# Three of the eight blocks of a second matmul computed from split operands, with GpSimd taking the difference

## The chip, the cores and the metric

The kernel runs on one core of a Trainium2 chip. The metric is the device time in microseconds (us) of one execution, the median of several runs; lower is better.

## The reference

Three stages follow one another. A gated linear attention with complex decay makes 3072 rows of 384 numbers. A dense mixture turns each row x into `(h * cos(h)) @ w_out` with `h = x @ w_in`. A second mixture sends each row to the one of eight experts that has the largest logit.

```python
def _moe_ref(x, w_in, w_out):
    h = x @ w_in                    # 384 -> 2048
    g = h * np.cos(h)
    return (g @ w_out).astype(np.float32)   # 2048 -> 384
...
    logits = x @ w_gate
    e_idx = np.argmax(logits, axis=1)
...
        h = np.maximum(x[mask] @ w1[e], 0.0)
        ye = h @ w2[e]
        out[mask] = gate_w[mask, None] * eom[mask, e, None] * ye
```

The change touches `g @ w_out`, the second matmul of the first mixture. Its output also feeds an argmax, so it is computed close to full fp32 precision.

## The kernel before

**Units.** The 3072 rows are worked in 12 units u = 0 to 11 of 256 rows. For each unit the kernel runs a scan (`scan`, on VectorE with ScalarE's help: `normal`, `core`, `inverse`, `post`), the attention (`attn`, TensorE with VectorE), and the first mixture. The loop over units interleaves them: while unit u is in the mixture, `attn(u + 1)` and `scan(u + 2)` are pulled forward piece by piece. Units 10 and 11 have no scan left to run, and unit 11 no attention. After unit 11 the experts follow (`second`).

**The mixture of one unit** has eight steps s = 0 to 7, each 256 of the 2048 columns. Step s does:

- `mm1(u, s)` (L508): h for these columns, 18 matmuls with a moving tile of 256 columns. Both operands are split there already, each into a high part in the reduced type fp32r and a low part, and three products are added (high*high, high*low, low*high). The PSUM tile h has two buffers.
- `act2(u, s)` (L516 to L518): three ScalarE activations from h to the SBUF tile g, 128 x 512.
- `act3(u, s)` (L523): VectorE makes g ready, reading g from SBUF and h from PSUM. After it the buffer of h is free, so `mm1(u, s + 2)` waits for it.
- `mm2(u, s - 2)` (L534): the second matmul, two steps later. For two halves of 128 rows and two groups of 128 columns it multiplies g by wo, 4 matmuls in plain fp32 with 400 moving columns (384 outputs and 16 logits); the trace shows each as two records, 8 in a block.

After the last block of a unit, `evac` (L557) copies the sums out, and one unit later `routing` finds each row's expert and scatters the rows with four indirect DMAs on GpSimd's queue (L541).

**GpSimd** does little before the change: once per unit twelve small operations on the carried state (`gates`, L204 and L344 to L353, right after the last operation of `core`), the scatters, and in the first 90 us eight subtractions that split w_in (`split`, the tile wi).

**Order.** A scheduler with a model of times sets the order on each engine from the order of the program and priorities (`tc.high_priority`); each engine then runs its list strictly in that order. Tiles come from pools with a fixed number of buffers: the pool gx, which holds g, has five.

Of the kernel before, what the change touches and what calls it, by code (L numbers as in the profile page):

```python
# [10 lines left out]
F32 = mybir.dt.float32  # L11
F32R = mybir.dt.float32r
# [10 lines left out]
C = 128  # L23
NCB = S // C
NCH = B * NCB
UC = 2
NU = NCH // UC
UPB = NCB // UC
NT = B * S
DM = H * D  # L30
DFF = 2048
KF = DFF // 128
NE = 8
NL = 2 * NE
# [6 lines left out]
NO = DM + NL  # L41
# [5 lines left out]
KP = KF // 2  # L47
NWC = 2 * KP + 1
NB = 2 * NU + 2 * NWC + NU * KF // 2 + NE
MAXH = 39.0  # L50
LAST = 6
EARLY = 5
# [82 lines left out]
def build(tc, ap, out, force=False):  # L135
# [4 lines left out]
    def pool(name, bufs=1, **kw):  # L140
        return tc.tile_pool(name=name, bufs=bufs, **kw)
# [4 lines left out]
    moe_ctx = ExitStack()  # L146
    wp = moe_ctx.enter_context(pool("wp", side="right"))
    xp = moe_ctx.enter_context(pool("xp", 2, side="right"))
    gx = moe_ctx.enter_context(pool("gx", 5, side="right"))
    rowp = moe_ctx.enter_context(pool("rowp", 2, side="right"))  # L150
    attn_ctx = ExitStack()
    qkrp = attn_ctx.enter_context(pool("qkrp", 2, side="left"))
# [50 lines left out]
    def tt(e, o, a, b, op):  # L203
        return e.tensor_tensor(out=o, in0=a, in1=b, op=op)  # L204
# [293 lines left out]
    NS = KF // 2  # L498
# [22 lines left out]
    def act3(u, s):  # L521
        g = gxt[u, s]
        V.scalar_tensor_tensor(out=g, in0=g, scalar=1.0, in1=hps.pop((u, s)), op0=SUB, op1=MUL)  # L523

    def mm2(u, s):
        g = gxt.pop((u, s))
        if s == 0:
            o_t[u] = [ps_o.tile([128, 512], F32, name=f"o{j}") for j in range(UC)]
        for j in range(UC):
            o = o_t[u][j][:, 0:NO]  # L530
            for i in range(2):
                f = 2 * s + i
                cs = slice(j * C, (j + 1) * C)
                PE.matmul(o, lhsT=g[:, i, cs], rhs=wos[s][:, i], start=f == 0, stop=f == KF - 1)  # L534

    rows_t = {}
    scat = {"xs": [], "xs0": [], "out": []}
# [16 lines left out]
    def evac(u):  # L554
        rows_t[u] = rowp.tile([128, UC, ROW], F32, name="rows")
        for j in range(UC):
            mark["evac"] = A.activation(out=rows_t[u][:, j, 0:NO], in_=o_t[u][j][:, 0:NO], func=AF.Copy, scale=-1.0)  # L557
        G.tensor_copy(rows_t[u][:, :, NO].bitcast(I32), ids[:, u * UC:(u + 1) * UC])
# [117 lines left out]
    def split(j):  # L676

        if j < KP:
            w = wp.tile([128, 2, 3, 256], F32R, name="wi", tag=f"w{j}")
            wis[j] = w  # L680
            t = wraw[j][0][..., 0].bitcast(F32)
            hi, lo = (w[:, r].rearrange("p a c -> p (a c)") for r in range(2))
            A.copy(hi, t)
            tt(G, lo, t, hi.bitcast(F32), SUB)
        else:
            w = wp.tile([128, 2, NO], F32, name="wo", tag=f"w{j}")
            wos[j - KP] = w
            if len(wraw[j]) == 1:
                r = wraw[j][0].rearrange("p (i c) t -> p i c t", i=2)
                parts = [(w[..., 0:DM], r[..., 0]), (w[..., DM:NO], r[:, :, 0:NL, 1])]  # L690
            else:
                parts = [(w[:, i, 0:DM], wraw[j][i][..., 0]) for i in range(2)]
                parts += [(w[:, i, DM:NO], wraw[j][i][:, 0:NL, 1]) for i in range(2)]
            for w, t in parts:
                A.copy(w, t.bitcast(F32))

    def gated(j):

# [26 lines left out]
    def run(g):  # L725
        for _ in g:
            pass
# [452 lines left out]
    if True:  # L1180
        load_a(0)
        SY.dma_start(ident, ap["cst"])
        SY.dma_start(cb, ap["msk"])
        SY.dma_start(smt, ap["sm"])
        SY.dma_start(ids, ap["ids"])
        SY.dma_start(rkt, ap["rk"])
        SY.dma_start(wg, ap["wg"].rearrange("(k p) l -> p k l", p=128))
        V.memset(pv_t, 0.0)
        V.tensor_copy(acc, smt[:, 1, 0])
        G.tensor_copy(top, smt[:, 3])  # L1190
        V.memset(eb, 0.0)
        V.memset(one[:, 0], 1.0)
        V.memset(one[:, 1], 0.0)
        nl = 11
        load_w(0, 1)
        load_qk(0)
        load_w(1, nl)
        n0 = 3

        run(scan(0))  # L1200
        load_w(nl, 2 * KP)
        run(weights(range(n0)))
        with tc.issue_after(mark["add", 0].ins):
            run(weights(range(n0, n0 + 2)))
        with tc.issue_after(mark["post", 0].ins):
            run(weights(range(n0 + 2, KP)))
        run(normal(1))
        run(attn(0))
        run(weights(range(KP, KP + EARLY)))
        with tc.high_priority(offset=100):  # L1210
            run(core(1))
            run(inverse(1, None))
        with tc.high_priority(offset=100):
            run(post(1))
        for u in range(NU):
            ga = attn(u + 1) if u + 1 < NU else iter(())
            gs = scan(u + 2) if u + 2 < NU else iter(())
            if u == 0:
                run(ga)
                gs = chain((normal(2), scan(2)))  # L1220

            def pull(g, n):
                for _ in range(n):
                    if next(g, StopIteration) is StopIteration:
                        return

            if u == NU - 2:
                scan_ctx.close()
            if u == NU - 1:
                attn_ctx.close()  # L1230
                open_early()
                for i in range(4):
                    stage(0, i)
                gs = split_w(0)
                gf = None

            for s in range(NS):
                mm1(u, s)
                if u == 0 and s >= EARLY:
                    with tc.issue_after(mark["add", 1].ins):  # L1240
                        run(weights([KP + s]))
                pull(ga, 2)
                pull(gs, 1)
                i = u * NS + s - 2
                if i >= 0:
                    mm2(*divmod(i, NS))
                    if i % NS == NS - 1:
                        with tc.high_priority(offset=300):
                            evac(i // NS)
                act2(u, s)  # L1250
                pull(ga, 1)
                pull(gs, 3)
                with tc.high_priority(offset=50):
                    act3(u, s)
                if s == 4 and u > 2:
                    routing(u - 1)
                    if u == NU - 1:
                        gf = first_half()
                if u == NU - 1 and s >= 4:
                    next(gf)  # L1260
                if s == NS - 1 and 0 < u < 3:
                    routing(u - 1)
            run(ga)
            run(gs)
        for s in range(NS - 2, NS):
            mm2(NU - 1, s)
        with tc.high_priority(offset=300):
            evac(NU - 1)
        with tc.high_priority(offset=100):
            routing(NU - 1)  # L1270
        run(gf)
        moe_ctx.close()
        ps_ctx.close()
        second()
# [21 lines left out]
```

## Time and profile before

| | |
|---|---|
| Median of 3 runs | 987.12 us (986.64 to 987.8) |
| Profiled execution, its own time | 988.75 us |
| Profiled execution, span from first to last instruction | 986.9 us |
| Busy in the span: TensorE / VectorE / ScalarE / GpSimd | 906.4 / 649.9 / 562.1 / 140.8 us |
| L534, second matmul of the first mixture | 768 records, 279.4 us busy |
| L508, first matmul of the first mixture | 1728 records, 250.8 us busy |
| Mean granted TensorE clock | 0.995 of full speed |

Busy time is a sum over the instructions of an engine. TensorE's instructions overlap, and their ends are modelled, so the durations of its records are longer than the time from one to the next; what a matmul costs is read from the chain of waits, where every piece ends where the next begins.

### The profile page before, as it was taken

To read this page: it belongs to the slowest core of one execution; us is meant where nothing else is said; L and a number is where in the kernel's file an instruction comes from. 1 tells how busy PE (TensorE), PEld (TensorE's weight loads), DVE (VectorE), ACT (ScalarE), POOL (GpSimd) and SP (SyncE) were. 2 spreads that over 40 slices of the span, in tenths; PEclk is the share of its full clock that TensorE was granted. 3 is DMA by queue.
4 is the path that set the end of the run, shared out by engine and by line. 5 is a ranking of instruction groups with operands and counts; after the bars stand their busy time and mean duration, and the time that the engine had idled before them with its cause. 6 is when DMAs were issued, how large, how long until landed. Compare 5 with 4: busy or idle time off the path is not lost.

```text
span 986.9 us, 16112 instructions
## 1 busy us (share of the span) xinstructions
PE 906.4 (92%) x5689; PEld 754.8 (76%) x5689; DVE 649.9 (66%) x1466; ACT 562.1 (57%) x1217; POOL 140.8 (14%) x254
## 2 busy tenths in 40 slices
PE   0467899999989999999999999999999999999997
PEld 0356677767768787778787777787789899999997
DVE  6988877696869796878889787334244554255521
ACT  6584875837484947586766655335454454255521
POOL 1122001002022002011212021101111110212101
PEclk9999999999999999999999999999999999999999
DMA  9713135336323333232424141342217542454101
GB/s 325 305 34 93 40 107 188 85 96 212 106 70 119 76 99 86 89 98 84 113 73 113 68 134 26 93 139 87 79 34 255 164 160 61 143 179 141 34 13 35
DMA packets 69790, 109.93 MB, mean 111 GB/s; under 512 B 14064, under 2 KB 51328, under 8 KB 69429
## 3 DMA queue, kind: packets, MB, share of 16 engines
q1 hardware_dynamic: 62724, 98.72, 32.3%
q0 software_dynamic: 6976, 10.10, 3.0%
q8 instruction: 47, 0.77, 0.3%
q14 instruction: 43, 0.34, 0.1%
HBM read 74.20 MB, written 21.86 MB: 97 GB/s over the span
## 4 chain that ended last, share of the span: by engine, by line
PE 43%; DVE 26%; ACT 10%; issue 8%; DMA 7%; SPq 6%; POOL 0%; DVEq 0%; ACTq 0%; POOLq 0%
PE p L933 11%; PE h L918 10%; PE o L534 9%; PE h L508 7%; DVE t L204 4%; DVE qkt L204 4%; DVE l_t L204 2%; DVE g L523 2%; DVE pt L204 2%; DVE nt L204 1%; SPq L368 1%; DMA qkr<-qkt 1%; DMA a_t<-in_a_dram 1%; ACT g L516 1%; SPq L371 1%
## 5 line engine op out<-in xcount | busy, mean ns | idle before, releaser
L534 PE MATMUL o<-wo,g 128*128 128x400 f32 x768 | 279.4, 505 | 0.5 <-ACT rows L557 0.5
L508 PE MATMUL h<-x,wi 128*128 128x256 f32 x1728 | 250.8, 297 | 19.5 <-DVE g L523 11.7
L508 PEld LDWEIGHTS h<-x,wi 128*128 128x128 f32 x1728 | 220.5, 192 | 40.7 <-DVE g L523 12.2
L534 PEld LDWEIGHTS o<-wo,g 128*128 128x128 f32 x768 | 138.4, 191 | 85.9 <-issue 4.1
L933 PE MATMUL p<-w2t,hh 128*128 128x384 f32 (+4 forms) x672 | 131.7, 341 | 0.0
L918 PE MATMUL h<-xe,w1t 128*128 128x384 f32 (+6 forms) x576 | 118.5, 349 | 0.0
L922 DVE SCALAR_TENSOR_TENSOR hh<-h,hh 128x384 fp32r<-128x384 f32 (+6 forms) x64 | 37.2, 583 | 121.1 <-ACT hh L921 121.1
L933 PEld LDWEIGHTS p<-w2t,hh 128*128 128x128 f32 (+4 forms) x672 | 114.0, 179 | 3.6 <-ACT hh L921 0.4
L516 ACT ACTIVATE g<-h 128x512 f32<-128x512 f32 x96 | 57.1, 595 | 104.7 <-PE h L508 104.4
L921 ACT ACTIVATE hh<-h 128x384 fp32r<-128x384 f32 (+6 forms) x64 | 32.8, 514 | 128.0 <-PE h L918 119.5
L918 PEld LDWEIGHTS h<-xe,w1t 128*128 128x128 f32 x576 | 101.7, 188 | 5.2
L523 DVE SCALAR_TENSOR_TENSOR g<-g,h 128x512 f32<-128x512 f32 x96 | 65.5, 682 | 57.0 <-ACT g L518 53.1
L541 POOL DMA_INDIRECT xs<-rows,si x46 | 53.1, 1154 | 195.4 <-DVE si L588 88.8
L518 ACT ACTIVATE g<-g 128x512 f32<-128x512 f32 x96 | 61.1, 636 | 2.0
L437 PE MATMUL sc<-qkr 96*128 96x128 f32 x384 | 55.7, 291 | 5.1 <-DMA qkr<-qkt 5.0
L437 PEld LDWEIGHTS sc<-qkr 96*128 96x128 f32 x384 | 50.8, 203 | 12.3 <-issue 5.1
L517 ACT ACTIVATE g<-h 128x512 f32<-128x512 f32 x96 | 57.7, 601 | 1.9
L541 POOL DMA_INDIRECT out_dram<-o,tok x28 | 35.4, 1265 | 145.7 <-ACT o L943 81.4
L204 POOL TENSOR_TENSOR fg<-l_t,m 128x12 f32<-128x12 f32 x24 | 4.6, 213 | 326.5 <-DVE l_t L204 248.3
L204 DVE TENSOR_TENSOR t<-l_t,a_t 128x192 f32<-128x192 f32 x144 | 46.7, 363 | 1.5
L707 PE MATMUL o<-ident,raw 128*128 128x128 f32 x30 | 8.4, 435 | 37.1 <-DVE raw L665 36.6
L204 DVE TENSOR_TENSOR qkt<-l_t,qk_t 128x1536 f32<-128x1536 f32 (+1 forms) x26 | 41.2, 1631 | 0.2
(277 smaller groups left out, 1351.0 us busy)
## 6 DMA issues: line engine op xcount, KB each, us to landing
stg<-in_w_dram SPq DMA_DIRECT2D x32, 768.0 KB
qkr<-qkt SPq DMA_DIRECT2D x96, 146.2 KB
a_t<-in_a_dram SPq DMA_DIRECT2D x12, 768.0 KB
qk_t<-in_qk_dram SPq DMA_DIRECT2D x12, 768.0 KB
xs<-in_xz_dram SPq DMA_DIRECT2D x17, 401.0 KB
raw<-in_w_in_dram SPq DMA_DIRECT2D x7, 768.0 KB
raw<-in_w_out_dram SPq DMA_DIRECT2D x7, 768.0 KB
vt<-in_v_dram SPq DMA_DIRECT2D x24, 192.0 KB
```

Source lines behind the costliest of these rows:

```text
L204: return e.tensor_tensor(out=o, in0=a, in1=b, op=op)
L437: PE.matmul(sc[:, h], lhsT=t[:, h, 1, 0:C], rhs=t[:, h, 0, 0:C], start=True, stop=True)
L508: PE.matmul(h[:, i], lhsT=wis[s][:, wi, kk, i * 128:(i + 1) * 128], rhs=x_t[u][:, xi, kk], start=n == 0, stop=n == 8)
L516: A.activation(out=g, in_=h, func=AF.Square, accum_out=hck[:, u * NS + s:u * NS + s + 1])
L517: mark["sin"] = A.activation(out=g, in_=h, func=AF.Sin, scale=0.5)
L518: A.activation(out=g, in_=g, func=AF.Square, scale=float(np.sqrt(2.0)))
L523: V.scalar_tensor_tensor(out=g, in0=g, scalar=1.0, in1=hps.pop((u, s)), op0=SUB, op1=MUL)
L534: PE.matmul(o, lhsT=g[:, i, cs], rhs=wos[s][:, i], start=f == 0, stop=f == KF - 1)
L541: sc = G.indirect_dma_start(in_offset=None, oob_is_err=False, **kw)
L918: PE.matmul(h, lhsT=w[:, wi, kk, f * 128:(f + 1) * 128], rhs=x[:, xi, kk], start=n == 0, stop=n == 8)
L922: mark["rest"] = V.scalar_tensor_tensor(out=hh[:, 1], in0=h, scalar=0.0, in1=hh[:, 0].bitcast(F32), op0=ALU.max, op1=SUB)
L933: mm = PE.matmul(o2[e][j][0:w_, 0:DM], lhsT=hh[:, hi, j * w_:(j + 1) * w_], rhs=w[:, wi, f], start=f == 0 and n == 0, stop=f == KE - 1 and ...
```

## The change

Blocks 2, 4 and 6 of each unit take the split path. A new step `act4`, one step after `act3`, copies g to a high part `ghi` in fp32r on ScalarE and lets GpSimd subtract it from g, which gives the low part `glo`. The weights of these three blocks are split as well, once, with VectorE making the low part. In `mm2` each of the 4 matmuls of such a block becomes three: high*high, high*low and low*high. The pool gx gets a sixth buffer; ghi and glo come from it too.

```diff
+SPLIT = (2, 4, 6)
...
-    gx = moe_ctx.enter_context(pool("gx", 5, side="right"))
+    gx = moe_ctx.enter_context(pool("gx", 6, side="right"))
...
+    def act4(u, s):
+
+        if s in SPLIT:
+            g = gxt[u, s]
+            hi = gx.tile([128, 2, UC * C], F32R, name="ghi", tag="g")
+            lo = gx.tile([128, 2, UC * C], F32R, name="glo", tag="g")
+            A.copy(hi, g)
+            tt(G, lo, g, hi.bitcast(F32), SUB)
+            gxt[u, s] = hi, lo
...
-                PE.matmul(o, lhsT=g[:, i, cs], rhs=wos[s][:, i], start=f == 0, stop=f == KF - 1)
+                if s not in SPLIT:
+                    PE.matmul(o, lhsT=g[:, i, cs], rhs=wos[s][:, i], start=f == 0, stop=f == KF - 1)
+                    continue
+                for n, (p, wi) in enumerate(((0, 0), (0, 1), (1, 0))):
+                    PE.matmul(o, lhsT=g[p][:, i, cs], rhs=wos[s][:, wi, i], start=f == 0 and n == 0,
+                              stop=f == KF - 1 and n == 2)
...
+            for i, c, t in parts:
+                A.copy(w[:, i, c], t.bitcast(F32))
+                if two:
+                    tt(V, wl[:, i, c], t.bitcast(F32), w[:, i, c].bitcast(F32), SUB)
...
+                if i >= -1:
+                    with tc.high_priority(offset=50):
+                        act4(*divmod(i + 1, NS))
                 act2(u, s)
```

On TensorE, in unit 8 of the changed kernel (o_5379 and o_5380 are the two halves of its output), a split block stands between two runs of the first matmul:

```order
L509 MATMUL h<-x,wi 128x256 x18
L549 MATMUL o_5379<-wo,ghi 128x400 x2
L549 MATMUL o_5379<-wo,glo 128x400
L549 MATMUL o_5379<-wo,ghi 128x400 x2
L549 MATMUL o_5379<-wo,glo 128x400
L549 MATMUL o_5380<-wo,ghi 128x400 x2
L549 MATMUL o_5380<-wo,glo 128x400
L549 MATMUL o_5380<-wo,ghi 128x400 x2
L549 MATMUL o_5380<-wo,glo 128x400
L509 MATMUL h<-x,wi 128x256 x18
```

Every block of the kernel before has in this place two rows of two matmuls that read g; the order of the blocks is the same.

On ScalarE, the end of one scan (`inverse` is `qkt<-l_t`, `qkt<-nt` and `qkt<-qkt`; `put_gates`, which opens `post`, is `qkt<-fg`) against the steps of the mixture, in unit 9 of the kernel before, right after the evacuation of unit 8:

```order
L557 ACTIVATE rows<-o_5086 128x400
L243 ACTIVATE qkt<-l_t 128x1536
L516 ACTIVATE g,hck<-h 128x512
L517 ACTIVATE g<-h 128x512
L247 ACT_TABLE_LOAD
L247 ACTIVATE qkt<-nt 128x768
L518 ACTIVATE g<-g 128x512
L248 ACTIVATE qkt<-qkt 128x768
L465 CAST x<-pv_t 128x4x128
L357 COPY qkt<-fg 128x24
```

and in unit 9 of the changed kernel, where the copy to ghi is that of block 6:

```order
L244 ACTIVATE qkt<-l_t 128x1536
L517 ACTIVATE g,hck<-h 128x512
L518 ACTIVATE g<-h 128x512
L248 ACT_TABLE_LOAD
L248 ACTIVATE qkt<-nt 128x768
L519 ACTIVATE g<-g 128x512
L249 ACTIVATE qkt<-qkt 128x768
L532 CAST ghi<-g 128x512
L517 ACTIVATE g,hck<-h 128x512
L518 ACT_TABLE_LOAD
L518 ACTIVATE g<-h 128x512
L358 COPY qkt<-fg 128x24
```

The end of this scan has moved from steps 1 to 3 of unit 9 to its steps 5 to 7. In units 2 to 4 the last operation of `core` stands after `act3` of step 6 in the changed order, in unit 9 after that of step 5; before, it went from step 5 in units 2 and 3 to step 1 in unit 9.

On GpSimd, from the end of the gates in unit 5 of the changed kernel to the start of the next gates:

```order
L354 COPY fg<-fg 128x6
L205 TENSOR_TENSOR glo<-g,ghi 128x512
L574 COPY rows<-ids 128x2
L205 TENSOR_TENSOR glo<-g,ghi 128x512 x2
L557 DMA xs<-rows,si 4096x401
L557 DMA xs_122<-rows,si 256x401
L557 DMA xs<-rows,si 4096x401
L557 DMA xs_122<-rows,si 256x401
L205 TENSOR_TENSOR fg<-l_t,m_132 128x12 x2
```

Before, `rows<-ids`, the gates and the four scatters were all that stood there. The subtractions of blocks 2 and 4 now stand ahead of the scatters and the gates, that of block 6 behind them.

## Rows read from the trace of the kernel before

**Rows 1.** Busy time by stage: start:end, length, busy us (x instructions) by engine, clock, DMA.

```profile
0.00:95.00 95.00, 44.35 (x214) 37.22 (x214) 80.15 (x138) 62.66 (x138) 19.50 (x25) 1.00 0.56 196
95.00:284.00 189.00, 171.21 (x1107) 135.42 (x1108) 143.18 (x324) 122.42 (x258) 18.73 (x60) 0.97 0.37 112
284.00:637.00 353.00, 346.47 (x2365) 271.68 (x2364) 282.74 (x652) 226.07 (x483) 53.26 (x119) 1.00 0.32 92
637.00:730.00 93.00, 93.00 (x558) 70.30 (x556) 31.29 (x81) 44.53 (x103) 8.16 (x10) 1.00 0.25 86
```

**Rows 2.** The chain of waits by line: stage 95:284, then 284:637, then 637:730.

```profile
by line: issue 8.3%; PE h L508 6.9%; DVE t L204 5.9%; DMA a_t<-in_a_dram 5.7%; PE o L534 5.2%; DMA xs<-in_xz_dram 3.9%; DVE qkt L204 3.4%; ACT g L516 3.0%; DVE g L523 2.6%; DMA ss<-s__2050 2.5%; DMA ss<-s__831 2.5%; ACT g L517 2.5%; SPq L49
...
by line: issue 10.6%; DVE qkt L204 7.9%; PE o L534 7.7%; DVE t L204 6.4%; PE h L508 5.5%; DVE g L523 5.0%; DVE l_t L204 4.1%; DVE pt L204 3.1%; DMA qkr<-qkt 2.7%; SPq L368 2.6%; DVE nt L204 2.6%; SPq L371 2.0%; ACT L517 1.8%; SPq L488 1.6%;
...
by line: PE o L534 52.6%; PE h L508 34.8%; PE sc L437 3.8%; PE pv_t L456 2.3%; PE pv_t L461 2.3%; PE m L472 1.4%; PE h L870 0.8%; PE sc L422 0.7%; PE sc L852 0.7%; PE m L422 0.6%; PE m L604 0.1%; PE m L585 0.1%; PE m L582 0.0%; PE m L584 0.
```

**Rows 3.** Pieces of that chain: start, us on the chain, engine, tile, line.

```profile
679.84 2.12 PE h L508 x18
681.96 2.69 PE o L534 x8
...
897.09 1.64 PE h L918 x9
```

**Rows 4.** Timeline of TensorE at 897 us, the shape of the piece at 897.09.

```profile
896.93 1.80 PE L918 MATMUL h<-xe,w1t 128*128 128x400 f32 x9
```

**Rows 5.** Waits over the whole span: us in total, times, longest.

```profile
DVE g L523 <- ACT g L518: 53.1, 27, 5.4
...
PE h L508 <- DVE g L523: 11.7, 5, 4.7
```

**Rows 6.** Timeline: gates of the scans 4 and 11, first activation of units 3 and 10.

```profile
271.51 0.20 POOL L344 COPY eb<-l_t 128x12 f32<-128x12 f32 x1
...
599.70 0.20 POOL L344 COPY eb<-l_t 128x12 f32<-128x12 f32 x1
...
283.58 0.58 ACT L516 ACTIVATE g<-h 128x512 f32<-128x512 f32 x1
...
636.93 0.60 ACT L516 ACTIVATE g<-h 128x512 f32<-128x512 f32 x1 [2.83 <-PE h L508]
```

**Rows 7.** Timeline of GpSimd: four of its eight subtractions for wi.

```profile
15.21 2.21 POOL L204 TENSOR_TENSOR wi<-raw,wi 128x768 fp32r<-128x768 f32 x1 [9.13 <-ACT wi L683]
...
26.75 1.99 POOL L204 TENSOR_TENSOR wi<-raw,wi 128x768 fp32r<-128x768 f32 x1 [1.25 <-ACT wi L683]
...
82.95 1.87 POOL L204 TENSOR_TENSOR wi<-raw,wi 128x768 fp32r<-128x768 f32 x1 [1.95 <-ACT wi L683]
85.86 1.85 POOL L204 TENSOR_TENSOR wi<-rawx,wi 128x768 fp32r<-128x768 f32 x1 [1.04 <-ACT wi L683]
```

**Rows 8.** Timeline of VectorE at three of these subtractions.

```profile
15.63 3.40 DVE L204 TENSOR_TENSOR a_t<-a_t,nt 128x1536 f32<-128x1536 f32 x1
...
27.07 1.88 DVE L204 TENSOR_TENSOR l_t<-t 128x192 f32<-128x192 f32 x1
...
87.02 1.10 DVE L204 TENSOR_TENSOR tp<-s__452,ss 96x384 f32<-96x384 f32 x1
```

**Rows 9.** VectorE's operations by tile: durations min/median/max in ns, first and last start.

```profile
L204 DVE TENSOR_TENSOR a_t<-a_t,nt x12: 1750/1758/3402, 15.6 to 572.9; 128x1536 f32<-128x1536 f32 x12
...
L204 DVE TENSOR_TENSOR l_t<-t x84: 341/357/1883, 23.4 to 588.3; 128x192 f32<-128x192 f32 x84
...
L204 DVE TENSOR_TENSOR tp<-s__508,ss x1: 544/544/544, 141.1 to 141.1; 96x384 f32<-96x384 f32 x1
...
L204 DVE TENSOR_TENSOR nt<-a_t,nt x12: 946/954/960, 6.7 to 548.8; 128x768 f32<-128x768 f32 x12
```

**Rows 10.** ScalarE's copies of a 128 x 512 tile from SBUF to fp32r, by tile.

```profile
L766 ACT CAST w1t<-stg x48: 610/622/628, 675.3 to 929.3; 128x512 fp32r<-128x512 f32 x48
```

**Rows 11.** Timeline of VectorE: a small two-operand operation.

```profile
764.90 0.18 DVE L204 TENSOR_TENSOR ex<-rt,pick 128x32 f32<-128x32 f32 x1
```

More of the change, by code (lines that the diff above doesn't have):

```diff
@@ L685, in split @@
         else:
-            w = wp.tile([128, 2, NO], F32, name="wo", tag=f"w{j}")
+            two = j - KP in SPLIT
+            w = wp.tile([128, 2, 2, NO], F32R, name="wo", tag=f"w{j}") if two else wp.tile([128, 2, NO], F32, name="wo", tag=f"w{j}")
             wos[j - KP] = w
+            if two:
+                wl, w = w[:, 1], w[:, 0]
             if len(wraw[j]) == 1:
                 r = wraw[j][0].rearrange("p (i c) t -> p i c t", i=2)
-                parts = [(w[..., 0:DM], r[..., 0]), (w[..., DM:NO], r[:, :, 0:NL, 1])]
+                parts = [(slice(0, 2), slice(0, DM), r[..., 0]), (slice(0, 2), slice(DM, NO), r[:, :, 0:NL, 1])]
             else:
[L692 to L695, printed above, removed]
+                parts = [(i, slice(0, DM), wraw[j][i][..., 0]) for i in range(2)]
+                parts += [(i, slice(DM, NO), wraw[j][i][:, 0:NL, 1]) for i in range(2)]
+            for i, c, t in parts:
+                A.copy(w[:, i, c], t.bitcast(F32))
+                if two:
+                    tt(V, wl[:, i, c], t.bitcast(F32), w[:, i, c].bitcast(F32), SUB)
     def gated(j):
@@ L1264, in build @@
             run(gs)
+        act4(NU - 1, NS - 1)
         for s in range(NS - 2, NS):
```

## The prediction

> **What bounds the kernel now.** I read the table of stages first. TensorE is busy for 44 of the first 95 us, for 171 of the next 189 (units 0 to 2), for 346.5 of 353 in units 3 to 9, and for all 93 us of units 10 and 11 [rows 1]. A full row of busy time does not yet say that TensorE sets the end, so I read the chain of waits by line next. In 637:730 it is TensorE and nothing else, L534 alone holding 52.6%. In 284:637 it is mixed: L534 has 7.7% and L508 5.5%, and the rest is mostly VectorE's scan (the tiles qkt, t, l_t, nt) with ScalarE and DMA. In 95:284 it is mixed too, L534 having 5.2% [rows 2]. The reader should see two things: from unit 10 on, time taken off L534 comes off the end one for one; before that, TensorE and the loop through VectorE are about equally long, since both are nearly without slack.
>
> How much slack the scan has in units 3 to 9 can be read from two pairs of starts. Its gates come at 271.51 and seven scans later at 599.70, so one scan takes 46.9 us; the first activations of units 3 and 10 are at 283.58 and 636.93, so one unit takes 50.5 us [rows 6]. The scan ran 3.6 us faster per unit than the mixture, and got ahead.
>
> **The change, part by part.**
>
> *TensorE.* A block of L534 takes 2.69 us on the chain [rows 3]. Twelve fp32r matmuls take its place. The expert with 400 rows gives the price directly: nine matmuls of L918 with a moving tile of 128 x 400 [rows 4] take 1.64 us on the chain [rows 3], 0.182 each, so 12 take 2.19 us. Each split block saves 0.50 us, 36 of them 18.0 us, if TensorE sets the end everywhere. L508 keeps its 2.12 us [rows 3]. The Trainium skill (FP8 and Floating Point Precision, TensorE Precision Notes) counts four passes for true FP32; three products in place of four passes would save a quarter, an estimated 0.67 us a block and 24 us in all. The rows say less, and the sum goes by the rows.
>
> Where the saving lands:
>
> - Units 10 and 11, 6 blocks: the chain is TensorE alone, so 3.0 us come off in full.
> - Units 3 to 9, 21 blocks: 10.5 us if the scan keeps up, nothing if it doesn't.
> - Units 0 to 2, 9 blocks: 4.5 us of work, but L534 is 5.2% of that stage's chain, 9.8 us [rows 2]. Three of eight of its blocks by 0.50/2.69 is 0.7 us; I take 0.5.
>
> *ScalarE.* 36 copies of 128 x 512 at 0.62 us [rows 10] are 22 us. ScalarE is busy for 226 of 353 us in units 3 to 9 [rows 1]; with 21 copies, 13 us, it stays under 70%. The copy must wait for `act3` on VectorE and holds up the next step's activations behind it. But those wait for the next `mm1`, whose end is a run of L508 and a block of L534 after that of the last, 4.8 us [rows 3], and in the units with attention more. I cost the copies at nothing. If that cover is gone, they cost up to their 0.62 each, 13 us in units 3 to 9.
>
> *GpSimd.* The trace has no subtraction of 512 elements. One of 768 took 1.85 to 1.87 us where little stood against it [rows 7], so by size 1.25 us, and with a fixed part rather more; I take 1.3 us, 47 us in all. GpSimd is busy for 53 of 353 us in units 3 to 9 [rows 1], and 27 more fit. Its list is strict, so `glo` stands in line: those of blocks 2 and 4 ahead of the scatters and the gates, that of block 6 behind them in unit 5. The block that needs it comes behind the L508 run of step s + 2, which itself waits for `act3` of step s. If TensorE is already waiting there, as it did five times [rows 5], 2.12 us of L508 [rows 3] cover 0.62 + 1.3 = 1.9 us of copy and subtraction; otherwise a block and a run more, 4.8 us, lie between. I cost the queue at nothing; what is late first, if this cover is gone, is block 6, behind the gates.
>
> *VectorE, the hidden price.* While GpSimd subtracts, VectorE's operations with two SBUF inputs stand still. The product a_t at 15.63 took 3.40 us where its median is 1.76, ending after the subtraction that began at 15.21; the sum l_t at 27.07 took 1.88 where its median is 0.36, ending with the one that began at 26.75; the product tp at 87.02 took 1.10 against 0.54 [rows 7 to 9]. Over the eight subtractions, the first and last of which are shown, VectorE lost 8.75 us by such excess, in 17.1 us of GpSimd's work: half of it. The Trainium skill (SBUF — State Buffer on-chip working memory, Who interferes with whom) has the rule behind it: a VectorE instruction with two SBUF inputs and a GpSimd instruction that reads SBUF exclude each other, and the second to issue blocks until the first is done. The trace agrees.
>
> So a `glo` of 1.3 us costs VectorE 0 (when it is waiting anyway, or reads PSUM) to 1.3 us; I take half, 0.65. That is 2.0 us in each unit that still has a scan, 19.5 us over units 0 to 9. VectorE is busy for 283 of 353 us in units 3 to 9 [rows 1], 40.4 us of each 50.5; it would be 42.4 of about 49. Part of this falls into time in which it now waits, 53 us in all for ScalarE ahead of L523 [rows 5]. Of the 14 us in units 3 to 9 between 0 and 14 can reach the end; the scan's lead of 3.6 us per unit is the nearest row and is larger than 2.0 plus the 1.5 that TensorE gains, though barely. And the order shows that the scan is given that lead no more: it ends in step 6 or 7 of each unit. I take 30%, 4.2 us.
> In units 0 to 2 the scan has no lead. Nine subtractions cost VectorE 5.9 us there, of which 0 to 5.9 reach the end. VectorE's lines that the rows of 284:637 still show are 29% of that chain, with many small ones cut off [rows 2]; I take 40% of the 5.9, 2.3 us.
>
> *The split weights.* Three more operations of 128 x 768 on VectorE at 0.95 us [rows 9] and three small ones at 0.18 [rows 11], 3.4 us, before and in unit 0, where VectorE is busy for 80 of 95 us [rows 1]. Between 0 and 3.4 us reach the end; I take a little over half, 1.9.
>
> *The sixth buffer* costs nothing: a split block draws three buffers, but each is given back by a matmul or a subtraction that is over before the sixth draw after it.
>
> **The sum.** -3.0 - 10.5 + 4.2 - 0.5 + 2.3 + 1.9 = -5.6 us. Against the profiled execution's own 988.75 us that is 983.1; the median stands 1.6 us below that execution, so **981.5 us**.
>
> **The rivals.**
>
> *All of it arrives.* The scan's waits shrink as fast as the lock lengthens it, and TensorE sets the pace from unit 3: the 4.2 is gone and half of the 4.2 us of early costs too, -11.9 us, about **975**. For it: TensorE is busy for 98% of units 3 to 9. Against it: the chain there runs over VectorE.
>
> *The lock makes VectorE the bound.* From unit 0 to 9 nothing of TensorE's saving counts, and the loop through VectorE grows. Its place is the scan in step 3 (`normal`, then `core`), 5 and 7 of each unit, where nearly every operation has two SBUF inputs; it decides when lock and other additions exceed the scan's lead, 3.6 us a unit, less the 1.5 us by which the mixture speeds up: 2.1 us, and I already expect 2.0. With VectorE on 40% of the chain, 40% of 19.5 us is 7.8; with 1.9 for the weights and -3.0 from the last two units it comes to +6.7 us, **994**. For it: the chain [rows 2], and L508 already waits 11.7 us for L523 [rows 5]. Against it: VectorE is only 80% busy.
>
> *They cancel.* Saving and lock are of one size in units 0 to 9, and what the last two units gain goes to the weights: **987**, within 0.2%.
>
> *The split is not cheaper.* If the matmuls took turns with weight loads worse than those of L918 do, a block would stay at 2.69 us and only the costs would remain, about 995. L918 loads new weights for each of its matmuls too, so this gets little.
>
> **How the numbers follow.** 0.2% is 2.0 us, about what a measurement of this kernel can tell from no change. The forecast's case (977 to 985) gets 0.46, all of it arriving 0.16, cancelling 0.14, VectorE as the bound 0.22, the split that is not cheaper 0.02. So faster is 0.62, same 0.14, slower 0.24. The range runs from 973 (all arrives, and units 0 to 2 give a little) to 994 (the lock as the bound); the likeliest case's own range is 977 to 985.
>
> **What would show it.** Right: L549 at about 2.19 us per split block on the chain; 36 subtractions of 1.3 to 1.7 us on GpSimd; operations such as t<-l_t,a_t and l_t<-t with maxima near 1.7 us all through 100 to 630 us, and VectorE's busy share in units 3 to 9 up from 80% to about 86%; one unit of the mixture at 49.5 to 50 us. Units 10 and 11 together 3 us shorter. Wrong: TensorE waiting for L524 or for qkr by several us per unit in units 3 to 9, gates that come 51 us apart or more, or matmuls of L549 that wait for glo behind the gates.

## The result: 0.7% slower, and the profile after

The median of 8 runs is 993.8 us (992.63 to 996.4), beside 987.8 of the kernel before on the same chip: a ratio of 1.0069, 95% interval [1.0055, 1.0082], so 6.8 us slower (here and below a ratio is turned into us on the 987.1 of before). The forecast was 981.5, 5.6 us faster than before, with a range up to 994: the time lies just inside the range, and the direction is wrong. The profiled execution took 996.2 us itself.

The head of the page, then busy time by stage as in [rows 1]:

```profile
span 994.3 us, 16481 instructions
...
PE 901.7 (91%) x5833; PEld 789.8 (79%) x5833; DVE 670.7 (67%) x1472; ACT 581.6 (58%) x1255; POOL 190.6 (19%) x290
```

```profile
0.00:95.00 95.00, 44.33 (x214) 37.11 (x214) 82.32 (x142) 63.06 (x138) 21.46 (x25) 1.00 0.57 195
95.00:284.00 189.00, 170.45 (x1141) 146.28 (x1142) 149.94 (x322) 128.91 (x268) 31.01 (x67) 0.95 0.37 111
284.00:637.00 353.00, 337.31 (x2400) 284.14 (x2400) 284.69 (x644) 228.01 (x493) 78.51 (x140) 0.98 0.31 87
637.00:730.00 93.00, 91.05 (x596) 76.55 (x595) 38.96 (x85) 51.75 (x114) 18.49 (x18) 0.98 0.33 107
```

In 284:637 TensorE stands idle for 15.7 us where it stood 6.5, and its granted clock is 0.98 instead of 1.00; VectorE is busy for 20.8 us more over the span (649.9 before). Busy time on the page is not the sum of the durations: time in which two instructions of an engine overlap counts once. The pieces of the chain of waits in unit 11 (start, us on the chain) have both kinds of block side by side, as in [rows 3]:

```profile
691.28 2.69 PE o L546 x8
...
696.20 2.18 PE o L549 x12
698.38 2.12 PE h L509 x18
```

The price of a split block was right, 2.18 us for 2.19. (By the four passes that the Trainium skill counts, FP8 and Floating Point Precision, TensorE Precision Notes, it would have been an estimated 2.02; the rows gave the price, not the count.) The new operations by tile (min/median/max in ns), and then one of the scan's small ones, before and after:

```profile
L205 POOL TENSOR_TENSOR glo<-g,ghi x36: 1265/1292/2051, 119.3 to 728.0; 128x512 fp32r<-128x512 f32 x36
...
L532 ACT CAST ghi<-g x36: 600/620/709, 118.6 to 727.3; 128x512 fp32r<-128x512 f32 x36
```

```profile
L204 DVE TENSOR_TENSOR t<-pb,l_t x72: 188/202/211, 33.7 to 592.5; 128x24 f32<-128x24 f32 x72
```

```profile
L205 DVE TENSOR_TENSOR t<-pb,l_t x72: 190/202/1307, 33.4 to 627.1; 128x24 f32<-128x24 f32 x72
```

Both durations came as predicted, and an operation of 0.2 us that never took over 0.211 in the kernel before now takes 1.307 at its longest, about as long as one subtraction. That is the lock, in the units as well; the rule that the prediction cited from the Trainium skill (SBUF — State Buffer, Who interferes with whom) holds here too.

The gates of scans 4 and 11 and the first activations of units 3 and 10, in the timelines of GpSimd and ScalarE:

```profile
276.26 0.20 POOL L345 COPY eb<-l_t 128x12 f32<-128x12 f32 x1
...
634.13 0.19 POOL L345 COPY eb<-l_t 128x12 f32<-128x12 f32 x1
```

```profile
281.95 0.58 ACT L517 ACTIVATE g<-h 128x512 f32<-128x512 f32 x1
...
644.11 0.60 ACT L517 ACTIVATE g<-h 128x512 f32<-128x512 f32 x1 [0.32 <-PE h L509]
```

A scan takes (634.13 - 276.26)/7 = 51.1 us where it took 46.9, a unit 51.7 where it took 50.5 [rows 6]. The waits, in us, times, longest, for [rows 5]:

```profile
DVE g L524 <- ACT g L519: 58.3, 25, 6.3
```

```profile
PE h L509 <- DVE g L524: 16.9, 10, 4.1
```

```profile
ACT ghi L532 <- DVE g L524: 21.9, 16, 3.2
```

The last is new: ScalarE stands at its copy, with all that is behind it in its list. In units 3 to 9 alone, TensorE's L509 waits for this `act3` 10.4 us in six places, where it waited 1.6 in one; that is most of what TensorE stands idle there.

### The profile page after: what moved, and what is told of

It is laid out like the page before. It is cut to its first block, busy times and chain, and to the rows that moved or that the text cites. A ratio compares the mean times of both kernels' runs of the same rounds, so it can differ in the third digit from the quotient of the medians.

```text
span 994.3 us, 16481 instructions
## 1 busy us (share of the span) xinstructions
PE 901.7 (91%) x5833; PEld 789.8 (79%) x5833; DVE 670.7 (67%) x1472; ACT 581.6 (58%) x1255; POOL 190.6 (19%) x290
## 4 chain that ended last, share of the span: by engine, by line
PE 43%; DVE 21%; ACT 13%; DMA 8%; issue 8%; SPq 7%; POOL 0%; ACTq 0%; DVEq 0%; POOLq 0%
PE p L954 11%; PE h L939 10%; PE h L509 7%; PE o L546 6%; DVE t L205 4%; DMA a_t<-in_a_dram 3%; PE o L549 2%; DVE qkt L205 2%; DVE l_t L205 2%; DVE pt L205 2%; SPq L369 2%; SPq L372 2%; DVE g L524 2%; ACT g L518 1%; PE sc L438 1%
## 5 line engine op out<-in xcount | busy, mean ns | idle before, releaser
L509 PE MATMUL h<-x,wi 128*128 128x256 f32 x1728 | 252.9, 298 | 28.2 <-DVE g L524 16.9
L509 PEld LDWEIGHTS h<-x,wi 128*128 128x128 f32 x1728 | 226.4, 197 | 46.4 <-DVE g L524 18.4
L546 PE MATMUL o<-wo,g 128*128 128x400 f32 x480 | 176.5, 506 | 0.0
L546 PEld LDWEIGHTS o<-wo,g 128*128 128x128 f32 x480 | 86.5, 192 | 51.3 <-issue 3.7
L205 POOL TENSOR_TENSOR glo<-g,ghi 128x512 fp32r<-128x512 f32 x36 | 49.1, 1364 | 403.9 <-ACT ghi L532 384.9
L524 DVE SCALAR_TENSOR_TENSOR g<-g,h 128x512 f32<-128x512 f32 x96 | 65.5, 682 | 61.5 <-ACT g L519 58.3
L549 PE MATMUL o<-wo,ghi 128*128 128x400 f32 x288 | 78.0, 357 | 3.0 <-ACT ghi L532 3.0
L557 POOL DMA_INDIRECT xs<-rows,si x46 | 49.6, 1077 | 60.8 <-DVE si L604 29.6
L549 PEld LDWEIGHTS o<-wo,ghi 128*128 128x128 f32 x288 | 52.3, 193 | 4.9 <-ACT ghi L532 4.2
L549 PE MATMUL o<-wo,glo 128*128 128x400 f32 x144 | 49.5, 355 | 0.8 <-POOL glo L205 0.8
## 6 DMA issues: line engine op xcount, KB each, us to landing
raw<-in_w_out_dram SPq DMA_DIRECT2D x7, 768.0 KB, 13.2
```

The source lines that it names most:

```text
L509: PE.matmul(h[:, i], lhsT=wis[s][:, wi, kk, i * 128:(i + 1) * 128], rhs=x_t[u][:, xi, kk], start=n == 0, stop=n == 8)
L549: PE.matmul(o, lhsT=g[p][:, i, cs], rhs=wos[s][:, wi, i], start=f == 0 and n == 0, stop=f == KF - 1 and n == 2)
L557: sc = G.indirect_dma_start(in_offset=None, oob_is_err=False, **kw)
```

## The experiments

All are compared with the kernel before in the same rounds. Three parts had to be told apart: TensorE's saving, the copy on ScalarE, the lock on VectorE. A fourth came to light on the way: each edit also moves the scheduler's order, above all the place of the scan in the units. On VectorE, the last operation of `core` in unit 9 stands behind the `act3` of step 1 in the kernel before and in the runs with the copy without its wait, the weights alone and (both) the last two units; of step 2 with the copy alone, copy and subtraction, the lock alone and the split alone with the scan early; of step 5 in the changed kernel, with two fills, with VectorE's own operation and with the whole change and the scan early; of step 6 in the other six. Runs of the first two groups have a scan that is early, the others one that is late, and a difference between the two kinds holds the order's price too.

### The copy and the lock, in the kernel before

**The copy alone.**

```diff
+            hi = gx.tile([128, 2, UC * C], F32R, name="ghi", tag="g")
+            A.copy(hi, g)
```

> The kernel before, with only the copies of the change added: in steps 2, 4 and 6 ScalarE copies g to ghi, one step after act3, and nothing reads ghi; no subtraction, no split weights, all blocks in plain fp32; gx has six buffers. If VectorE blocked by GpSimd's reads is the cause of the loss (theory lock), this is within 2 us of the kernel before, 987.8 us. If it is the copy, which waits in ScalarE's list for act3 and holds the scan's activations behind it (theory copy), it is 4 us or more slower, 992 or above, and VectorE's waits for ScalarE in the inverse grow as they did in the changed kernel (from 28 to 42 us).

Measured: 1.0063 [1.0042, 1.0084], 6.2 us slower. The waits of ScalarE:

```profile
ACT ghi L531 <- DVE g L524: 40.8, 20, 4.4
```

VectorE's waits for ScalarE in the inverse hardly grew, though (30.9 us for 28.1), so what the held list delays is not shown.

**Copy and subtraction**, with the blocks still in plain fp32.

```diff
             A.copy(hi, g)
...
+            tt(G, lo, g, hi.bitcast(F32), SUB)
```

> As the run before it, with GpSimd's subtraction added too; nothing reads glo, all blocks stay in plain fp32. The order on every engine is almost that of the copies alone, so the difference between the two is the subtraction by itself. Theory lock: VectorE's busy time grows by about 20 us, and the time by 6 to 12 us over the copies alone. Theory copy: within 1.5 us of the copies alone.

Measured: 1.0182 [1.0151, 1.0212], 18.0 us slower, 11.8 more than the copy alone, with nearly the same order of the work. VectorE is busy for 669.0 us; with the copy alone it was 647.8.

**The copy without its wait**, against the copy alone: it reads a weight tile that is long there.

```diff
-            A.copy(hi, g)
+            ci = A.copy(hi, wos[0][:, :, 0:UC * C])
+            behind(ci, ("act3", u, s))
```

> As the copies alone (first run), but each copy reads a weight tile that has long been there in place of g: the same work on ScalarE, without the wait for act3; nothing reads the copy. The scheduler may place things differently since the wait is gone. If the wait of ScalarE for VectorE is what the copies cost (theory wait), this is within 2 us of the kernel before, 985 to 989. If it is ScalarE's 22 us of work (theory work), it is as slow as the copies alone, 992 to 994.

Measured: 1.0007 [0.9989, 1.0024]: no difference. The page has the copies' work, but not their price (ScalarE 562.1 us before):

```profile
PE 905.1 (92%) x5689; PEld 755.3 (77%) x5689; DVE 650.4 (66%) x1466; ACT 582.8 (59%) x1255; POOL 142.5 (14%) x254
```

20.7 us more work on ScalarE cost nothing; the same copies cost 6.2 us where they wait for `act3`. The order moved a little with it, so the wait and what it does to the order go together in that figure.

**The lock alone, and an operation of VectorE's own.** A product that nothing reads, behind the `act3` of steps 2, 4 and 6, on GpSimd in one run and on VectorE, `tt(V, ...)`, in the other:

```diff
+        if s in SPLIT:
+            dm = gx.tile([128, 2, UC * C], F32, name="dm", tag="g")
+            tt(G, dm, g, g, MUL)
```

> The kernel before with a GpSimd product of g by itself (128x512, read by nothing) behind each block of steps 2, 4 and 6: GpSimd reads SBUF 36 times, as in the changed kernel, but ScalarE copies nothing and waits for nothing. VectorE should be blocked for some 20 us in all. If the blocks of units 0 to 9 go in step with VectorE's list, three quarters of that reach the end, as with an operation of its own: 13 to 17 us slower than before, 1001 to 1005 us. If the prediction's share holds: 6 to 8 us slower, 994 to 996 us.

> The kernel before with one more VectorE operation (128x512, a product of g by itself that nothing reads) behind each block of steps 2, 4 and 6: 36 of about 0.68 us, some 24 us on VectorE, with no wait of another engine for it. This measures what share of an addition to VectorE reaches the end. The prediction took 30 to 40 per cent: 7 to 10 us slower than before, 995 to 998 us. If the blocks of units 0 to 9 go in step with VectorE's list: 15 to 24 us slower, 1002 to 1011 us.

On GpSimd: 1.0104 [1.0073, 1.0134], 10.3 us slower. On VectorE: 1.0199 [1.0168, 1.023], 19.6 us slower. Of each the page and the tile:

```profile
PE 912.3 (92%) x5689; PEld 758.7 (76%) x5689; DVE 663.1 (67%) x1466; ACT 564.5 (57%) x1219; POOL 189.5 (19%) x290
```

```profile
L205 POOL TENSOR_TENSOR dm<-g x36: 1032/1086/2287, 118.8 to 727.8; 128x512 f32<-128x512 f32 x36
```

```profile
PE 916.5 (91%) x5689; PEld 765.5 (76%) x5689; DVE 667.7 (66%) x1502; ACT 563.3 (56%) x1219; POOL 140.4 (14%) x254
```

```profile
L205 DVE TENSOR_TENSOR dm<-g x36: 678/684/693, 121.8 to 738.4; 128x512 f32<-128x512 f32 x36
```

GpSimd's 36 operations make VectorE 13.2 us busier (663.1 against 649.9), and 10.3 us, 78% of it, reach the end (55 to 100% by the interval): between the two cases expected, and above the 30 to 40% of the prediction. VectorE's own 36 are 24.6 us by their durations and, where they overlap with their neighbours, add 17.8 to its busy time (667.7). The end moves by 19.6, that is 80% of the one and 110% of the other; but this edit made the scan late, and the first did not, so part of the 19.6 may be the order's. The lock is paid for the larger part; that it is paid just as VectorE's own work is not shown.

### Taking the lock out of the changed kernel

**One fill in place of the subtraction.**

```diff
-            A.copy(hi, g)
-            tt(G, lo, g, hi.bitcast(F32), SUB)
+            ci = A.copy(hi, g)
+            mi = G.memset(lo.bitcast(F32), 0.0)
+            tc.add_manual_dep(mi.ins, ci.ins.name,
...
```

> The changed kernel with GpSimd's subtraction replaced by a memset of glo to zero, made to wait for the same copy, so GpSimd's list, the copies, the split weights and all matmuls stay and only GpSimd's reads of SBUF go; the low part of g is left out of the sums by this. Theory lock: 13 us less than the changed kernel's 993.8, about 981, and VectorE's busy time back by 15 to 20 us. Theory copy: above 990. If neither, and the scheduler's order alone keeps the scan back: between 986 and 991.

Measured: 1.0059 [1.0032, 1.0086], 5.8 us slower than before, where the changed kernel is 6.8 slower. Read by itself this says that the lock costs 1 us. But the fill is shorter than the subtraction, and the scheduler moved the work with it: the end of the scan stands in step 6 of every unit from 1 to 9, where the changed kernel has it in step 5 by unit 9 and the kernel before in step 1.

**Two fills**, with which the order stays nearly that of the changed kernel:

```diff
+            G.memset(lo.bitcast(F32), 0.0)
```

> The changed kernel with two fills of the low part by zeros on GpSimd in the place of the subtraction (so the low part of g is left out of the result). With two, GpSimd's list is held about as long as by one subtraction and the order of the work stays nearly that of the changed kernel, which it did not with a single fill; but nothing on GpSimd reads SBUF and VectorE isn't blocked. If the lock on VectorE is what costs, at the three quarters that an operation of VectorE's own pays: 978 to 984 us. If the copy's wait and the late scan cost it whatever the lock does, as with the single fill: above 990 us.

Measured: 0.9981 [0.9964, 0.9999], 1.9 us faster than before. Its page:

```profile
PE 897.5 (91%) x5833; PEld 786.3 (80%) x5833; DVE 651.0 (66%) x1472; ACT 581.4 (59%) x1255; POOL 179.3 (18%) x326
```

VectorE is 19.7 us less busy than in the changed kernel (670.7), the very size of the predicted 19.5, and the end comes 8.7 us sooner (6.5 to 10.9 by the two intervals): 44% of it was on the path (33 to 55%), with two fills of 0.526 us in GpSimd's list for one subtraction of 1.292. That too lies between the two cases expected. The single fill and the two fills give the same result; besides one more fill on GpSimd only the order differs, and 7.7 us lie between them.

### The split on TensorE alone

**The weights alone.** The blocks stay in fp32 and read the high part.

```diff
...
-                for n, (p, wi) in enumerate(((0, 0), (0, 1), (1, 0))):
-                    PE.matmul(o, lhsT=g[p][:, i, cs], rhs=wos[s][:, wi, i], start=f == 0 and n == 0,
-                              stop=f == KF - 1 and n == 2)
+                PE.matmul(o, lhsT=g[:, i, cs], rhs=wos[s][:, 0, i].bitcast(F32), start=f == 0, stop=f == KF - 1)
```

> The weights of the three blocks split and nothing else: the block's product stays in fp32 and reads the high part of the weights (their low part, which VectorE computes, is left out of the result). This is the term of 1.9 us, between 0 and 3.4, for 3.4 us more on VectorE before and in unit 0. If an addition to VectorE is paid at three quarters: 2.6 us. The order of the work is that of the kernel before but for a few places, so any larger difference would speak of order and not of work.

Measured: 1.0043 [1.0022, 1.0064], 4.2 us slower, above the 1.9 of the prediction and, within its interval, near the full 3.4 of VectorE's work.

**The split without copy and subtraction**: `act3` writes the block in fp32r.

```diff
...
+        if s in SPLIT:
+            hi = gx.tile([128, 2, UC * C], F32R, name="ghi", tag="g")
+            gxt[u, s] = hi, hi
+        V.scalar_tensor_tensor(out=hi, in0=g, scalar=1.0, in1=hps.pop((u, s)), op0=SUB, op1=MUL)
```

> The split on TensorE alone: VectorE writes the block of g at once in fp32r (the low part of g is left out, and the third product takes the high part again), so that twelve fp32r matmuls stand in the place of eight and the weights are split, but ScalarE copies nothing, GpSimd subtracts nothing and nothing is locked. The prediction's terms for this part are 3.0 + 10.5 + 0.5 saved less 1.9 for the weights: 12 us faster than before, 975 to 977 us. By what the other runs leave (6.8 slower, of which the lock 8.4 and the copies 6.2) the split with its weights is worth 7.8 us: 979 to 981 us. If units 0 to 9 take nothing of it, because VectorE's loop sets them: 984 to 986 us.

Measured: 0.997 [0.9952, 0.9989], only 3.0 us faster. In this order too the scan ends in step 6 of units 1 to 9.

**The same with the scan early.**

```diff
-                pull(gs, 3)
+                with tc.high_priority(offset=80):
+                    pull(gs, 3)
```

(and the same around the other `pull(gs, 1)`).

> The split on TensorE alone as in the run before (no copy, no subtraction; the low part of g is left out and the third product takes the high part again), with the scan's pieces at a higher priority. In that order the scan gains on the mixture as it does in the kernel before: its end stands in step 2 of unit 9, where the run before has it in step 6 of every unit. If the split's saving was lost to the late scan, it arrives: 12 us faster than before, 974 to 978 us. If the loop over VectorE takes half of it in any order: within 2 us of the run before, 982 to 986 us.

Measured: 0.9857 [0.983, 0.9885], 14.1 us faster. Stages of this run, and of the run before it:

```profile
95.00:284.00 189.00, 173.04 (x1183) 145.94 (x1183) 152.15 (x336) 131.45 (x287) 22.85 (x58) 0.97 0.38 115
284.00:637.00 353.00, 345.50 (x2509) 292.54 (x2508) 277.13 (x649) 229.53 (x483) 61.92 (x121) 1.00 0.34 97
637.00:730.00 93.00, 92.43 (x614) 79.76 (x613) 39.66 (x103) 47.70 (x101) 11.55 (x13) 1.00 0.27 88
```

```profile
95.00:284.00 189.00, 171.63 (x1164) 146.03 (x1165) 147.53 (x329) 127.76 (x270) 21.15 (x60) 0.95 0.36 112
284.00:637.00 353.00, 344.69 (x2460) 289.31 (x2458) 275.38 (x647) 228.55 (x483) 45.76 (x119) 0.99 0.31 88
637.00:730.00 93.00, 89.43 (x596) 75.23 (x595) 38.94 (x100) 44.23 (x103) 8.32 (x11) 1.00 0.33 103
```

The same instructions with another order end 11.1 us apart. With the scan early the idle time and the clock of TensorE are those of [rows 1], 24.0 us idle in 95:730 against 24.3, and the whole saving arrives. So the theory that VectorE's loop swallows TensorE's saving in units 0 to 9 falls: the order with the late scan did it. The same priority in the kernel before, whose scan is early already, was not run, so that a part of the 14.1 may be the priority's own.

**The whole change with the scan early.** The same edit in the changed kernel moves the scan by one step at most, in some of the units 2 to 7, and not at all in unit 9.

> The changed kernel, complete, with the scan's pieces at a higher priority, by which its end stands one step earlier in units 2 to 4 and 7 and at the same step in unit 9: most of the order stays. If the place of the scan decides, a small gain, 990 to 993 us; if the lock and the copies do, 993 to 997 us.

Measured: 1.0067 [1.0044, 1.009], as the changed kernel. So little of a move gains nothing; the whole change with the scan as early as before was not run.

### Other places for the copy

**The copy later**, behind `act2` of the next step and without priority; then the same with one fill for the subtraction.

```diff
-                if i >= -1:
-                    with tc.high_priority(offset=50):
-                        act4(*divmod(i + 1, NS))
                 act2(u, s)
+                if i >= -1:
+                    act4(*divmod(i + 1, NS))
```

> The changed kernel with ScalarE's copy of a block moved back in the program: written behind the gelu product's first half of the next block instead of ahead of it, and without its higher priority, so that the copy stands where its block has mostly been finished already. What is computed is the same. Theory 1 (what costs is ScalarE held at the copy until VectorE has finished the block, 21.9 us of wait in the changed kernel): most of that wait goes and the time is 983 to 988 us. Theory 2 (in units 0 to 9 the blocks run in a loop over TensorE, ScalarE and VectorE; what the change adds on VectorE, by the lock of the port and the split weights, is paid at its full length whatever ScalarE does): 992 us or more.

> The kernel before this one, and the subtraction on GpSimd replaced by filling the low part with zeros (so the low part of g is left out of the result): neither the wait on the copy nor the lock is left. If those two are all that the change costs, what is left is the split's own saving on TensorE, 18 us over 36 blocks, less the weights' 3.4: 975 to 982 us. If the order of the work in units 3 to 9, with the scan of the second mixture late in every unit, costs by itself: above 987 us.

Measured: 1.0152 [1.0123, 1.0182], 15.0 us slower, and 1.0113 [1.0081, 1.0146], 11.2 us slower. The wait went as meant:

```profile
ACT ghi L532 <- DVE g L524: 3.4, 5, 1.6
```

and the time rose all the same. Both orders have the scan's end in step 6 of nearly every unit; its gates come 52.4 and 53.0 us apart. So these two runs do not price the wait: the order moved with it, and cost more than the wait's end can have gained.

**The copy on VectorE**, with the subtraction, and with the fill.

```diff
-            A.copy(hi, g)
+            V.tensor_copy(hi, g)
```

> The changed kernel with ghi copied by VectorE in place of ScalarE, so that no ScalarE instruction waits for act3 any more; GpSimd's subtraction stays. VectorE gets 36 copies of 128 x 512, some 13 to 22 us. Theory wait: faster than the changed kernel by 4 us or more, 984 to 990. Theory lock alone: VectorE is the bound and gets more work, so 996 or above.

> As the run before it, with GpSimd's subtraction replaced by the memset of the third run (the low part of g is left out of the sums by this), so neither ScalarE's wait nor GpSimd's reads are there, while all matmuls and the split weights stay. If wait and lock together are the cause, the split's gain comes out: 975 to 982. If it stays above 987, a third thing holds units 0 to 9 back, such as the scheduler's order, or VectorE's load itself.

Measured: 1.0271 [1.0242, 1.0299], 26.7 us slower, and 1.0213 [1.0181, 1.0245], 21.0 us slower. The 36 copies of 0.418 us are 15 us of VectorE's time, and the first run is 20 us slower than the changed kernel; with them the scan's end moved to step 6 of every unit, so the figure holds the order too.

### Splitting only where TensorE alone sets the end

Seven of eight blocks, in units 10 and 11 only; their weights are split in unit 10, the subtraction is VectorE's, which has time there. First with the copy on ScalarE, as here, then on VectorE by `V.tensor_copy(hi, g)`:

```diff
+SPLIT = (1, 2, 3, 4, 5, 6, 7)
+FROM = NU - 2
...
+        if late(u, s):
...
+            A.copy(hi, g)
+            tt(V, lo, g, hi.bitcast(F32), SUB)
```

> A version that should beat both: seven of eight blocks split, but only in units 10 and 11, where no scan is left; the low part of g on VectorE, and the weights of these blocks split in unit 10 by copies through a spare tile (VectorE 14 and ScalarE 7 operations of 800 columns more). All theories say that the 14 blocks save 0.50 us each on TensorE's chain, 7 us, less what the new copies hold up: 981 to 984. If the price of a split block were not what the chain shows, it would stay at 987 to 988.

> The fourth run (seven of eight blocks split in units 10 and 11 alone) with ghi copied by VectorE in place of ScalarE. In its trace ScalarE's activations and a wait for x stood on the chain of unit 10. Theory wait: 1 to 2 us faster than the fourth run, 982 to 983.5. Otherwise the same, 984 to 985.

Measured: 0.9968 [0.9952, 0.9985], 3.2 us faster, and 0.9925 [0.9897, 0.9952], 7.4 us faster than before. The stages of the second:

```profile
284.00:637.00 353.00, 348.14 (x2358) 273.43 (x2358) 281.08 (x650) 224.61 (x479) 53.78 (x119) 0.99 0.32 92
637.00:730.00 93.00, 92.98 (x667) 85.94 (x666) 58.84 (x139) 54.02 (x119) 9.49 (x11) 1.00 0.26 86
```

Units 3 to 9 are those of the kernel before, and in 637:730 VectorE takes 27.6 us more than in [rows 1] while TensorE stays busy throughout. 14 blocks at 0.51 us are 7.1 us, and all of it arrives (4.7 to 10.2 by the interval). This version beats both kernels.

## Why the prediction was wrong

**The step that failed is the scan's lead of 3.6 us a unit, and with it the price of the subtraction and the copy in units 0 to 9.** On that lead the prediction took the saving of units 3 to 9 in full and the lock there at 30% ("I take 30%, 4.2 us"); with 40% in units 0 to 2 the lock came to 6.5 us, and the copies to nothing. In the new order 0.6 us of the lead are left: a scan takes 51.1 us, a unit 51.7. The changed kernel is 6.8 us slower for a forecast of 5.6 faster, so 12.4 us have to be found, and the runs add up to the 6.8 in two ways.

With an early scan: copy and subtraction cost 18.0 us together, 6.2 for the copies and 11.8 for the subtraction on top (10.3 for a lock alone). Against that stands the saving with its weights, 14.1 us: 18.0 - 14.1 = 3.9 us slower. The 2.9 left are within what the intervals of three runs leave open (1.3 to 3 us to a side each) and may be the late scan.

With the late scan, as in the changed kernel, each run against the one before it: the split alone saves 3.0, copies and two fills on top cost 1.1 (-1.4 to 3.6 by their intervals), and the subtraction in place of the fills 8.7. Here most of what the prediction missed is the saving that does not come, 3.0 for 12.1; the lock's 8.7 is only 2.2 above the 6.5.

So late scan, copies and lock are not separate sums: what one takes the other cannot take again. In both the lock costs more than the 6.5 of the prediction, 8.7 or 11.8 us, and with two fills in its place the changed kernel is 1.9 us faster than the one before. How the rest divides between the copies' wait and the late scan stays open.

Point by point:

- *The split block*, 2.19 us for 2.69: right (2.18). *What the split and its weights save together*, 12.1 us: right where the scan is early (14.1, interval 11.4 to 16.8), 3.0 where it is late.
- *Units 10 and 11, -3.0.* From the `act3` of the first step of unit 10 to the last one of unit 11 it is 85.2 us before and 84.2 after. Some 2 us went missing, since TensorE is no longer busy throughout (91.05 of 93 us, clock 0.98).
- *The size of the lock*, 19.5 us of VectorE: right (19.7 between the changed kernel and the one with two fills).
- *The share of it that reaches the end*, 33%: too low. It was 44% in the changed kernel, 56% on top of the copy and 78% by itself. The 33% stand at the lower end of the first figure's interval. The argument from the scan's lead was wrong: that lead goes with the order. The prediction saw the scan's end move to steps 5 to 7 and put no price on it.
- *The copies at nothing*: the named cover ("those wait for the next `mm1`") hides their work, as the copy without a wait shows, but not the wait for `act3`: 21.9 us in the changed kernel, 40.8 in the run with the copy alone. ScalarE's list also holds the scan's activations, and these have no such cover; that they are what costs is not shown. In the late order the copies and the two fills together cost 1.1 us (-1.4 to 3.6).
- *The weights*, 1.9 us: 4.2 [2.2, 6.3], so more than a little over half.
- *The rival "the lock makes VectorE the bound"* gave +6.7 us and 994, and 6.8 and 993.8 came. Its sign was right, and its terms come close to those of the late order: it let nothing of TensorE's saving count in units 0 to 9 and took 7.8 us for the lock, and there the runs give 3.0 with the weights for its 1.1, and 8.7. But its reason, that VectorE's loop swallows the saving, falls with the split alone: with the scan early all of it arrives. That the number came so near is partly luck.
- *What would show it*: gates 51 us apart or more were named as a sign that the forecast was wrong, and came. TensorE waiting for L524 was another, but by several us per unit: in units 3 to 9 it is 10.4 us, 1.5 per unit. L549 waiting for glo behind the gates, also named, did not: 0.8 us in three waits. Of the signs that it was right, VectorE's share in units 3 to 9 was to be 86%; it is 81% (284.69 of 353), since the units grew with it.

## What to carry to other kernels

In a stage where several engines run strict lists in step, ask of an added wait what stands behind it in that list, and price what blocks the engine that the scan runs on by half of its length or more (44 to 78% of the lock here), not by a third. When an edit lets a scheduler choose a new order, run the same work in the old order before believing any difference: order was worth 11.1 us here with the same instructions, and 7.7 with one fill between. And put a saving for one engine where that engine alone is the chain: 14 blocks in the last two units gave more than 36 everywhere.

## What was not expected

**TensorE's idle time can be paid a second time, in its clock.** The change leaves it 36.2 us idle in 95:730 instead of 24.3. Windows of 5 us, as in [rows 1], of the changed kernel:

```profile
130.00:135.00 5.00, 2.28 (x16) 1.66 (x14) 3.07 (x4) 5.00 (x18) 0.00 (x0) 0.99 0.55 132
135.00:140.00 5.00, 4.97 (x25) 4.96 (x26) 4.53 (x5) 4.16 (x13) 1.48 (x1) 0.50 0.44 113
140.00:145.00 5.00, 5.00 (x21) 4.97 (x21) 2.67 (x8) 0.61 (x3) 0.00 (x0) 0.50 0.66 209
145.00:150.00 5.00, 5.00 (x64) 4.95 (x63) 4.31 (x12) 0.51 (x1) 0.00 (x0) 0.98 0.10 32
```

and of the kernel before:

```profile
130.00:135.00 5.00, 3.33 (x18) 2.22 (x17) 2.60 (x3) 5.00 (x20) 0.00 (x0) 1.00 0.59 139
135.00:140.00 5.00, 4.92 (x43) 4.48 (x42) 3.71 (x4) 3.35 (x11) 0.00 (x0) 1.00 0.41 105
```

TensorE was busy for 2.28 of 5 us before 135; then the granted clock is 0.50 for ten us, the lower of its two levels (1.2 of 2.4 GHz). In the kernel before it was busy for 3.33 there, and the clock stayed at 1.00. The timeline of TensorE has the wait at which this began, for the copy, and a later one for `act3`:

```profile
135.03 1.70 PE L549 MATMUL o<-wo,ghi 128*128 128x400 f32 x4 [1.68 <-ACT ghi L532]
...
588.02 3.52 PE L509 MATMUL h<-x,wi 128*128 128x256 f32 x18 [4.05 <-DVE g L524]
```

After the second wait the run of 18 matmuls takes 3.52 us by its records (granted clock 0.61 over 588 to 592), where those of the run at 118.86 take 2.59 (granted clock 1.00). Multiplied out, (1 - clock) times busy over the 127 windows of 5 us from 95 to 730, the lower clock costs 15.4 us in the changed kernel and 4.4 before, 11.0 more, beside 11.9 of idle time. The 18 us that the split saves, less these two, make the last `act3` of the mixture some 5 us later; it is 7.2 later, at 732.1 against 724.9. In the split alone with the scan early both are as before, 4.3 and 24.0.

How much of this holds in the median is another matter, for these are two single executions, each from an edge. The changed kernel's mean clock of 0.980 is the lowest of its eight executions (median 0.984), and the 0.995 of the kernel before is reached by 4 of the 94 executions of it that were timed beside the experiments (0.974 to 0.998, median 0.989). Between the medians lies 0.005 and not 0.015, a third, so some 4 us (an estimate) in place of 11.0. Nor is there a fixed ratio: by the same count the run with two fills loses 11.6 us more to the clock than the kernel before beside 7.6 more of idle time, and copy and subtraction 4.5 beside 8.4.
